# Ten orders written out, one for each pair of feature tiles, in place of two orders and a rule

## The chip, the cores and the metric

The kernel runs on one core of one Trainium2 chip. The metric is the device time of one execution in microseconds (us), lowest median best. Every engine has its own queue and runs it in order: TensorE (PE in the profile) multiplies, VectorE (DVE), ScalarE (ACT) and GpSimd (POOL) do the elementwise work, SyncE (SP) issues the transfers. Semaphores tie them together.

## The reference

The input `x` has 2048 rows of 640 numbers. Two branches are computed from it and mixed by a gate for each row:

```
g = sigmoid((x * gate_w).sum(-1))
a = linear attention of x with 32 heads of 20: learned features (two softmaxes), o = num / den, a = o @ wo
b = silu(x @ w1) @ w2          # w1: 640 x 1728, w2: 1728 x 640
out = g * a + (1 - g) * b
```

All of it is fp32. The kernel splits each operand of a product into a high and a low part in a reduced format and adds three products (high by high, high by low, low by high), so a logical product of 128 x 128 by 512 columns is three matmuls.

## The kernel before, in words

The program is straight code without a loop on the chip. It runs in three phases: keys and values of the attention with the first part of the dense branch (to about 180 us of the profile); the dense branch `b` (about 180 to 510 us); queries, attention output and mixing (the rest). The change is in the second phase.

There the rows are taken in two halves of 1024 (`h`), each of two column blocks of 512 (`j`). The 1728 features are 13 tiles of 128 and a rest. Ten of the tiles form five pairs, and each pair is computed once for each half: ten pair times, numbered `n` = 0 to 9, and the outputs of pair time n are made during pair time n + 1. Pair time 10 takes the last outputs, and one more pair of tiles beside them. In the text "pair n" is that loop index `n`, and order n belongs to it.

`pair_mm` (first layer) makes a pair with fewer products than plain multiplication: sums and differences of weight blocks and of x blocks are formed first (the weights' by `pair_weights` in the first half, stored and loaded again by `pair_weights_again` in the second). It is a generator cut into pieces, a product and what follows it on the other engines:

- P1m, P5m, P6m, P7m, Cm: products into one bank a of the accumulator memory (PSUM), line 925; P2m, P4m, P3m: products into banks b, d, c.
- P1p and P6p: a copy of bank a by ScalarE (lines 947, 969). P5m adds to the bank that P1p copies.
- P5p, P3p, P7p, Cp: sums on VectorE (957, 958, 975, 988, 989), silu on ScalarE (939), the high half (940), then the low half by VectorE or GpSimd (941). The result is `u`.

The second layer has two forms. In pair times 1 to 5 and 10, `out_items` makes ten (or five) outputs: okm is six products into a bank (line 1014), oke adds the bank to an accumulator on VectorE (1019). There are four such banks, used in turn, so the fifth product group from here must wait for this eviction. In pair time 5 each oke is followed by a product with the gate on GpSimd (1088) and a store. In pair times 6 to 9, `sevens` makes the outputs with seven products in place of eight: pieces 1am to 7bm, y0m, y1m (1055, 1077) and evictions 1ae to 7be, y0e, y1e (1043, 1045); t2, t3, t4 are differences of `u` on GpSimd (909), h and l their high and low halves on ScalarE and GpSimd (899, 903).

Between them stand the preparations, also in pieces:

- w0 to w11 (`pair_weights`): w0 loads two raw tiles; w1 and w2 make high halves on ScalarE (313, 813) and low halves on GpSimd (324, 814); w3 to w6 are sums on GpSimd (823); w7 to w10 high and low halves of these (826, 827). In the second half w0 to w3 are loads alone (840).
- c0 to c3 (`w2_loads`): load, then high half on ScalarE (313) and low half on GpSimd (324), for each of two tiles of the second layer; in the second half c0 and c1 are loads (847).
- b0 to b8 and d0 to d8 (`block_sums`): four sums on GpSimd (879), four high halves on ScalarE (884) with low halves on VectorE (885).
- xl and xu, yl and yu: a load of x on SP (639), and its halves on ScalarE and VectorE (1341, 1342). In pair 4, r0 and r1 issue four loads of x each; s10 and s11 are differences on VectorE, s20 to s41 on GpSimd (773); p10 to p41 their halves on ScalarE (777) and VectorE (778). g loads the gates.
- s0, s1 in pairs 6 to 9: loads of stored sums (894). st: the stores that are due.

All instructions of TensorE, ScalarE, VectorE and GpSimd in this phase are held in the order in which the pieces are called (`inorder`), so a piece that waits holds up all that is behind it on its engine. SP's issues are placed by the framework, by written order and by readiness in its own schedule. Tiles with one tag share a few slots: raw tiles four, weights in tag w nine.

What sets the order of the pieces: pair 0 has an order written out, `HEAD`. For pairs 6, 7 and 8 there is `SLOT`, for pair 9 `LAST`. For pairs 1 to 5 and 10 there is a rule, `pair_time` with `emit`: after each piece pair of `pair_mm` it takes so many okm, oke as a table says (`PT`, `PTS`), and before and after each of these at least two preparations, or more if otherwise they would not be through in time. Followed by hand, the rule gives for pair 1

```
P1m P1p b0 b1 o0m o0e b2 b3 P2m P2p b4 b5 o1m o1e b6 b7 P5m P5p st b8 c0 o2m o2e c1 c2 P4m P4p c3
o3m o3e d0 d1 P6m P6p d2 d3 o4m o4e d4 d5 P3m P3p d6 d7 o5m o5e d8 w0 P7m P7p w1 w2 o6m o6e w3 w4
o7m o7e w5 w6 o8m o8e w7 w8 Cm Cp w9 w10 o9m o9e w11
```

and for pair 4

```
g P1m P1p c0 r0 o0m o0e c1 r1 P2m P2p c2 o1m o1e P5m P5p st s10 c3 o2m o2e s11 P4m P4p s30 w0 o3m
o3e s31 w1 P6m P6p s20 w2 o4m o4e s21 w3 P3m P3p s40 o5m o5e s41 p10 P7m P7p p11 p40 o6m o6e p41 xl4
o7m o7e xu4 p20 o8m o8e p21 xl3 Cm Cp xu3 o9m o9e
```

## Time and profile before

| what | value |
|---|---|
| median of 3 runs | 731.88 us (731.69 to 732.32) |
| the profiled execution | 732.16 us, span in the profile 730.4 us, clock 1.000 |
| TensorE busy | 722.1 us, 99% |
| VectorE busy | 429.7 us, 59% |
| GpSimd busy | 396.0 us, 54% |
| ScalarE busy | 297.1 us, 41% |
| transfers | 98.80 MB, mean 135 GB/s |

How to read it: the span runs from the first to the last instruction that the profile holds, and the execution's own time is 1.8 us longer. A row of the timeline is the start in us from the begin of the span, the length, the engine, the line of the kernel, the operation, what it writes and reads with the shapes, how many are merged in it, and in brackets the idle time of the engine before it and what ended it. Matmuls are pipelined: a row's length contains the drain of its last one, and the step from one start to the next tells the pace. The table of windows cuts the span where one asks for it and gives each engine's busy time in each piece.

### The profile page before, as it was taken

Reading aid. Unit: us, or ns where it says so; the run is one execution under the profiler, and the core shown is the slowest. Engines: PE = TensorE matmul, PEld = TensorE weight load, DVE = VectorE, ACT = ScalarE, POOL = GpSimd, SP = SyncE. Lnnn points to the kernel's source line nnn. Section 1 sums busy time; section 2 is a strip of 40 time slices with the busy share of each in tenths; the row PEclk is TensorE's granted clock in tenths of the full one; section 3 lists DMA queues with packets and bytes.
Section 4 is the critical chain, followed back from the end, with each engine's and each line's share of the span. In section 5 each row is a group of like instructions: output and inputs, shape, how many; then the busy total and the mean of one; then the engine's idle time right before and its main releaser. Section 6 shows DMA issues by size and latency. Waiting matters only on the chain.

```text
span 730.4 us, 12517 instructions
## 1 busy us (share of the span) xinstructions
PE 722.1 (99%) x4935; PEld 621.2 (85%) x4935; DVE 429.7 (59%) x708; ACT 297.1 (41%) x558; POOL 396.0 (54%) x307
## 2 busy tenths in 40 slices
PE   9999999999999999999999999999999999999998
PEld 8888888888888878887888788788997899999988
DVE  4565555565253546568625655663887776766652
ACT  5333322336465354435354323435334453435330
POOL 2354545534756385472866548311598767777440
PEclk9999999999999999999999999999999999999999
DMA  8111111114734567786965613342133322121222
GB/s 300 61 56 56 46 56 55 63 35 136 242 116 176 208 259 239 255 318 243 382 226 180 228 65 105 97 133 73 52 110 114 111 95 80 59 91 47 74 87 80
DMA packets 50751, 98.80 MB, mean 135 GB/s; under 512 B 6352, under 2 KB 25828, under 8 KB 50692
## 3 DMA queue, kind: packets, MB, share of 16 engines
q1 hardware_dynamic: 50692, 98.00, 39.6%
q8 instruction: 39, 0.64, 0.4%
q14 instruction: 20, 0.16, 0.1%
HBM read 66.15 MB, written 31.84 MB: 134 GB/s over the span
## 4 chain that ended last, share of the span: by engine, by line
PE 87%; POOL 5%; DVE 3%; issue 2%; ACT 2%; DMA 1%; SPq 0%; DVEq 0%; POOLq 0%; ACTq 0%
PE kvp L527 17%; PE o L1014 13%; PE pa L1636 10%; PE a L925 8%; PE pq L503 7%; PE o L1055 4%; PE ph L593 3%; PE c L925 3%; PE d L925 3%; PE b L925 3%; PE pn L1594 3%; PE pT L1487 2%; PE hp L612 2%; PE kvt L514 2%; PE o_m L1077 1%
## 5 line engine op out<-in xcount | busy, mean ns | idle before, releaser
L1014 PE MATMUL o<-u,w 128*128 128x512 f32 x580 | 142.8, 391 | 0.1
L1014 PEld LDWEIGHTS o<-u,w 128*128 128x128 f32 x580 | 108.0, 188 | 23.1 <-DVE acc L1019 0.9
L527 PE MATMUL kvp<-wh,xa 128*128 128x480 f32 (+2 forms) x420 | 92.4, 360 | 0.0
L527 PEld LDWEIGHTS kvp<-wh,xa 128*128 128x128 f32 x420 | 72.8, 188 | 10.4
L324 POOL TENSOR_TENSOR w<-wr,w 128x640 fp32r<-128x640 f32 x26 | 42.0, 1619 | 72.5 <-ACT w L313 64.6
L1636 PE MATMUL pa<-oT,wo 128*128 128x256 f32 x600 | 77.0, 281 | 0.1
L1636 PEld LDWEIGHTS pa<-oT,wo 128*128 128x128 f32 x600 | 73.8, 188 | 1.1 <-DVE oT L1615 0.8
L1170 POOL TENSOR_TENSOR ez<-eq,zbc 128x1280 f32<-128x1280 f32 x16 | 48.0, 3000 | 47.9 <-DVE sm L1200 24.6
L555 POOL TENSOR_TENSOR ek<-ek,st 128x1280 f32<-128x1280 f32 x16 | 38.2, 2386 | 50.4 <-DVE st L554 42.1
L1019 DVE TENSOR_TENSOR acc<-acc,o 128x512 f32<-128x512 f32 x70 | 46.5, 680 | 16.6 <-PE o L1014 16.4
L503 PE MATMUL pq<-wq,xb 128*128 128x320 f32 x360 | 55.9, 312 | 0.0
L939 ACT ACTIVATE v<-v 128x512 f32<-128x512 f32 x33 | 20.9, 632 | 84.6 <-DVE v L958 36.7
L503 PEld LDWEIGHTS pq<-wq,xb 128*128 128x128 f32 x360 | 52.9, 188 | 2.2 <-DVE oT L1615 2.0
L155 POOL TENSOR_TENSOR xa<-xra,xa 128x512 fp32r<-128x512 f32 (+1 forms) x26 | 26.3, 1036 | 41.7 <-ACT xa L153 37.3
L527 PE MATMUL kvp<-wl,xa 128*128 128x480 f32 (+2 forms) x210 | 47.5, 356 | 0.0
L1153 ACT ACTIVATE eq<-eq 128x1280 f32<-128x1280 f32 x16 | 20.4, 1277 | 63.6 <-DVE eq L494 63.6
L941 DVE TENSOR_TENSOR u<-v,u 128x512 fp32r<-128x512 f32 x29 | 21.2, 731 | 34.5 <-ACT u L940 30.2
L360 ACT COPY v<-kvp 128x340 f32<-128x340 f32 (+1 forms) x30 | 12.5, 417 | 70.2 <-PE kvp L527 68.3
L527 PEld LDWEIGHTS kvp<-wl,xa 128*128 128x128 f32 x210 | 36.6, 188 | 4.8
L1045 DVE TENSOR_TENSOR acc<-acc,o 128x512 f32<-128x512 f32 x48 | 31.3, 684 | 12.1 <-PE o L1055 12.1
L1206 POOL TENSOR_TENSOR eq<-eq,sm 128x1280 f32<-128x1280 f32 x16 | 37.9, 2366 | 1.0 <-DVE sm L1200 0.8
L553 DVE TENSOR_REDUCE st<-ek 128x64 f32<-128x1280 f32 x16 | 23.8, 1486 | 22.7 <-ACT ek L689 21.3
(236 smaller groups left out, 1485.5 us busy)
## 6 DMA issues: line engine op xcount, KB each, us to landing
wr<-w SPq DMA_DIRECT2D x33, 320.0 KB
w_d<-w SPq DMA_DIRECT2D x15, 640.0 KB
xr<-xT SPq DMA_DIRECT2D x27, 256.0 KB
w<-w_d SPq DMA_DIRECT2D x10, 640.0 KB
fb_d<-acc SPq DMA_DIRECT2D x20, 256.0 KB
s_d<-s SPq DMA_DIRECT2D x8, 512.0 KB
sa<-s_d SPq DMA_DIRECT2D x8, 512.0 KB
y<-fb_d SPq DMA_DIRECT2D x16, 256.0 KB
```

Source lines behind the costliest of these rows:

```text
L324: eng.tensor_tensor(t[:, 1, :], r[:, :D], t[:, 0, :].bitcast(F32), op=ALU.subtract)
L503: nc.tensor.matmul(dst, xt[c][:, hx, :], w[:, c, hw, lo : lo + n], start=first, stop=(hx == 1 and c == NC - 1))
L527: nc.tensor.matmul(kv_cols(t, lo, hi), xt[c][:, hx, :], WKV[hw][:, c, w_cols(lo, hi)], start=(n == 0), stop=(n == 3 * NC - 1), skip_group_ ...
L555: nc.gpsimd.tensor_tensor(groups(e), groups(e), spread(st[:, 1, :]), op=ALU.mult)
L925: last["mm"] = nc.tensor.matmul(out, lhs, rhs, start=(first and i == 0), stop=(stop and i == len(todo) - 1), skip_group_check=True)
L1014: nc.tensor.matmul(o, lhs, rhs, start=(n == 0), stop=(n == len(todo) - 1))
L1019: nc.vector.tensor_tensor(acc[j][m], acc[j][m], o, op=ALU.add)
L1045: nc.vector.tensor_tensor(acc[j][m], acc[j][m], o, op=ALU.add)
L1055: nc.tensor.matmul(o, ws[hw], x()[hx], start=(first and i == 0), stop=(i == len(PASSES) - 1), skip_group_check=True)
L1170: nc.gpsimd.tensor_tensor(ez, Q[t]["e"], zbc, op=ALU.mult)
L1206: nc.gpsimd.tensor_tensor(groups(q["e"]), groups(q["e"]), spread(q["sm"][:, 2 * H : 4 * H]), op=ALU.mult)
L1636: nc.tensor.matmul(pa[:, a, :], wo_tile[0][:, c, hw, ds] if c < NG else WOR[:, ds], o[:, ho, c, :] if c < NG else o[:GW, ho, c, :], start= ...
```

## The change

The rule and the two orders are gone; each pair from 1 to 10 has its own order of pieces, O1 to O10, and one loop calls the pieces in that order. The set of pieces of each pair is the same, and each piece does the same work on the same engine. Engine by engine, this is what stands in another order:

- Pair 1: on ScalarE d6 ahead of P3p, w1 ahead of P7p, w9 ahead of Cp; on VectorE d4 ahead of o4e, d6 ahead of P3p.
- Pair 2: on ScalarE w1, w2 ahead of P6p and w10 ahead of P7p; on VectorE d5 ahead of o2e.
- Pair 3: o1m ahead of P2m on TensorE; xu0, xu1 ahead of c1 and d5 ahead of P6p on ScalarE; xu0 ahead of o0e, d4 and d5 ahead of o3e and d7 ahead of o4e on VectorE; the loads xl in the order 2, 1, 0.
- Pair 4: c3 ahead of P5p, p10 ahead of P3p, p11 and p40 ahead of P7p, and xu3 ahead of Cp on ScalarE; on VectorE s10 ahead of o1e, p10 ahead of P3p's sum, p11 and p40 ahead of P7p, p41 ahead of o6e, xu4 ahead of o7e, xu3 ahead of Cp; r0 and g, p20 and p21 swapped; GpSimd's part of c3 comes with it, in the same place of its queue.
- Pair 5: P5p's sums ahead of o3e, and its low half ahead of o3's product with the gate; c0 ahead of yl3 and w0, w1 ahead of st on SP.
- Pair 6: y0m ahead of P5m on TensorE; P1p ahead of 2ae and h3 ahead of 1be on ScalarE; s1 ahead of c0 on SP.
- Pair 7: P5p ahead of h4 (ScalarE), y0e (VectorE) and l3 (GpSimd); s1 and w1 ahead of c0 on SP.
- Pairs 8 and 9: no engine's order changes.
- Pair 10: yu0 ahead of o1e and yu1 ahead of P5p.

```diff
@@ -78,17 +78,56 @@
 hp10 v1 hm11 hp11 hp13 v2 p21 v3 da4 P5m P5p P4m em0 p30 y0 v4 y1 y2 ea0 P4p em1 y3 P6m y4 ea1 y5 P6p
 em2 P3m y6 y7 ea2 P3p y8 y9 P7m P7p em3 Cm ea3 y10 em4 y11 Cp ea4
 """
-SLOT = """
-s0 P1m t3 w0 2am 1bm t2 2ae P1p 1am 1be 1ae 2bm h3 P2m h2 P2p t4 l2 c0 2be P5m y0m y0e s1 w1 l3 c1 h4
-P5p P4m y1m 6am w2 P4p P6m 6bm y1e 6ae P6p l4 6be 5am w3 5bm 5ae P3m 7am 5be P3p 7ae 7bm 7be P7m 4am
-3bm 4ae 3am P7p 3ae 4bm 3be Cm 4be Cp
+O1 = """
+P1m P1p o0m b0 b1 o0e b2 b3 P2m P2p b4 b5 o1m o1e b6 b7 P5m P5p st b8 c0 o2m o2e c1 c2 c3 P4m P4p d0
+o3m o3e d1 d2 P6m P6p d3 d4 o4m o4e d5 d6 P3m P3p d7 d8 o5m o5e P7m w0 w1 P7p w2 w3 o6m o6e w4 w5 o7m
+o7e w6 w7 o8m o8e w8 w9 Cm Cp w10 w11 o9m o9e
 """
-LAST = """
-P1m t3 1am t2 s0 w0 1bm s1 P1p 1be 2am P2m 2bm c0 P2p h2 1ae l2 h3 l3 2be P5m 6am t4 w1 h4 2ae P5p w2
-y0m w3 y1m y1e 6bm w4 P4m P4p l4 P6m y0e 6ae w5 w6 w7 5am 5ae P6p P3m 6be P3p 5bm c1 w8 5be 7am P7m
-7bm 7ae 7be 3am w9 4am P7p 3ae Cm 3bm Cp w10 4ae 3be 4bm w11 4be
+O2 = """
+P1m o0m P1p c0 c1 o0e c2 c3 P2m P2p d0 d1 o1m o1e d2 d3 P5m P5p st d4 d5 o2m o2e d6 d7 P4m P4p w0 o3m
+d8 o3e w1 P6m w2 P6p w3 w4 o4m o4e w5 w6 P3m P3p w7 w8 o5m o5e w9 w10 P7m P7p w11 o6m o6e o7m o7e o8m
+o8e Cm Cp o9m o9e
+"""
+O3 = """
+xl2 xl1 P1m P1p xl0 o0m c0 xu0 o0e o1m P2m o1e xu1 P2p c1 xu2 P5m st c2 P5p c3 o2m o2e d0 d1 P4m P4p
+d2 d3 o3m d4 d5 o3e P6m P6p o4m d6 d7 o4e d8 w0 P3m P3p w1 w2 o5m o5e w3 w4 P7m P7p w5 w6 o6m o6e w7
+w8 o7m o7e w9 o8m w10 o8e w11 Cm Cp o9m o9e
+"""
+O4 = """
+r0 P1m P1p o0m g c0 o0e c1 P2m P2p r1 c2 o1m st s10 o1e c3 P5m o2m P5p o2e s11 P4m w0 P4p s30 w1 o3m
+o3e s31 w2 P6m P6p s20 w3 o4m o4e s21 s40 P3m p10 P3p o5m s41 o5e p11 p40 P7m P7p p41 xl4 o6m o6e xu4
+o7m o7e p21 p20 xl3 o8m o8e xu3 Cm Cp o9m o9e
+"""
+O5 = """
+P1m P1p p30 p31 o0m o0e yl4 yu4 o1m o1e yl2 yu2 o2m o2e P2m P2p c0 yl3 yu3 c1 o3m w0 w1 P5m P5p st w2
+w3 o3e o4m o4e P4m P4p P6m P6p o5m o5e P3m P3p o6m o6e P7m P7p o7m o7e o8m o8e Cm Cp o9m o9e
+"""
+O6 = """
+s0 P1m t3 w0 2am 1bm t2 P1p 1am 2ae 1ae 2bm h3 1be P2m st h2 P2p t4 l2 y0m y0e s1 c0 2be P5m w1 l3 c1
+h4 P5p P4m y1m 6am w2 P4p P6m 6bm y1e 6ae P6p l4 6be 5am w3 5bm 5ae P3m 7am 5be P3p 7ae 7bm 7be P7m
+4am 3bm 4ae 3am P7p 3ae 4bm 3be Cm 4be Cp
+"""
+O7 = """
+P1m t3 s0 w0 2am t2 1bm P1p 2ae 1am 1be 1ae 2bm h3 P2m st h2 s1 w1 P2p t4 l2 c0 2be P5m c1 P5p y0m
+y0e l3 h4 P4m y1m 6am w2 P4p P6m 6bm y1e 6ae P6p l4 6be 5am w3 5bm 5ae P3m 7am 5be P3p 7ae 7bm 7be
+P7m 4am 3bm 4ae 3am P7p 3ae 4bm 3be Cm 4be Cp
+"""
+O8 = """
+s0 P1m t3 w0 2am 1bm t2 2ae P1p 1am 1be 1ae 2bm h3 P2m st h2 P2p t4 l2 c0 2be P5m y0m y0e s1 w1 l3 c1
+h4 P5p P4m y1m 6am w2 P4p P6m 6bm y1e 6ae P6p l4 6be 5am w3 5bm 5ae P3m 7am 5be P3p 7ae 7bm 7be P7m
+4am 3bm 4ae 3am P7p 3ae 4bm 3be Cm 4be Cp
+"""
+O9 = """
+t3 P1m 1am 1bm 1be t2 s0 w0 s1 2am P1p P2m st P2p 2bm c0 h2 1ae l2 h3 2be P5m l3 6am t4 w1 h4 2ae P5p
+w2 y0m w3 y1m y1e 6bm w4 P4m P4p l4 P6m y0e 6ae w5 w6 w7 5am 5ae P6p P3m 6be P3p 5bm c1 w8 5be 7am
+P7m 7bm 7ae 7be 3am w9 4am P7p 3ae Cm 3bm Cp w10 4ae 3be 4bm w11 4be
+"""
+O10 = """
+P1m P1p c0 c1 o0m o0e c2 c3 P2m P2p yl0 yu0 o1m o1e yl1 yu1 P5m P5p st q0 o2m q1 o2e kb kl P4m P4p
+o3m o3e P6m P6p o4m o4e P3m P3p P7m P7p fl0 Cm Cp
 """
 NSEV = 4
+ORDERS = (HEAD, O1, O2, O3, O4, O5, O6, O7, O8, O9, O10)
 PASSES = ((0, 0), (0, 1), (1, 0))
...
-    def emit(prep, k, slots, least=1):
-        for _ in range(max(least, -(-len(prep) // max(slots, 1)))):
-            if prep and prep[0][0] <= k:
-                prep.pop(0)[1]()
-
-    def pair_time(d1, d2, prep, counts):
-        slots = len(counts) + sum(counts)
-        for k, n in enumerate(counts):
-            twice(d1)
-            if k == 2:
-                store()
-            for i in range(n + 1):
-                emit(prep, k, slots, 2)
-                slots -= 1
-                if i < n:
-                    twice(d2)
-        run(d1)
-        emit(prep, len(counts), 1)
-        assert not prep
...
-    PT = (1, 1, 1, 1, 1, 1, 3, 1)
-    PTS = {NPAIR - 1: (3, 1, 1, 0, 1, 1, 2, 1), 2 * NPAIR - 2: (1, 1, 1, 1, 1, 0, 0, 0)}
...
-            prep = thunks((w2_again if again else w2_loads)(2 * p, 2 * p + 1), 5)
-            if NPAIR - 2 < n + 1 < 2 * NPAIR - 2:
-                prep += thunks(pair_weights_again(n + 1), 5)
-            elif n + 1 < 2 * NPAIR - 1:
...
+            q = (n - 1) % (NPAIR - 1)
+            ops["st"] = store
+            named(MM, pair_mm(n, h))
             if NPAIR - 1 < n < NPAIR + NSEV:
+                sevens(q, n == NPAIR)
+                named("s0 s1", sums_again(q))
+                for i in range(1, 4):
+                    ops[f"t{i + 1}"] = lambda i=i, q=q: t_sum(q, i)
+                    ops[f"h{i + 1}"] = lambda i=i, q=q: t_hi(q, i)
+                    ops[f"l{i + 1}"] = lambda i=i, q=q: t_lo(q, i)
+            else:
+                d2 = out_items(int(n > NPAIR - 1), (2 * q, 2 * q + 1), end=n == NPAIR - 1)
+                named(" ".join(f"o{k}m o{k}e" for k in range(2 * NC if n < 2 * NPAIR - 2 else NC)), d2)
+            if NPAIR - 2 < n < 2 * NPAIR - 2:
+                named("c0 c1", w2_again(2 * p, 2 * p + 1))
+            else:
+                named("c0 c1 c2 c3", w2_loads(2 * p, 2 * p + 1))
+            if NPAIR - 3 < n < 2 * NPAIR - 3:
+                named("w0 w1 w2 w3", pair_weights_again(n + 1))
+            elif n < 2 * NPAIR - 2:
+                named(" ".join(f"w{k}" for k in range(12)), pair_weights(n + 1))
             if n == 1:
+                named(" ".join(f"b{k}" for k in range(9)), block_sums(0))
             if n < NSEV:
+                named(" ".join(f"d{k}" for k in range(9)), block_sums(n))
             if n == NPAIR - 3:
+                new_chunks(0, "x", {c: lambda k=k: place(k) for c, k in ((0, 8), (1, 9), (2, 11))})
             if n == NPAIR - 2:
+                ops["g"] = lambda: load_gates(0)
+                for cc in range(2):
+                    ops[f"r{cc}"] = lambda cc=cc: half_raws(cc)
+                    for i in range(1, 5):
+                        eng = nc.vector if i == 1 else nc.gpsimd
+                        ops[f"s{i}{cc}"] = lambda i=i, cc=cc, eng=eng: x_sum(i, XR[cc], eng)
+                    for i in (1, 2, 4):
+                        ops[f"p{i}{cc}"] = lambda i=i, cc=cc: x_part(i, cc, XR[cc])
+                new_chunks(0, "x", {4: slot_of(0, 4), 3: lambda: place(10)})
             if n == NPAIR - 1:
+                for cc in range(2):
+                    ops[f"p3{cc}"] = lambda cc=cc: x_part(3, cc, XR[cc])
+                new_chunks(1, "y", {c: slot_of(1, c) for c in (4, 2, 3)})
             if n == 2 * NPAIR - 2:
-            pair_time(pair_mm(n, h), d2, prep, PTS.get(n, PT))
+                new_chunks(1, "y", {c: slot_of(1, c) for c in range(2)})
+                named("q0 q1", reg_loads())
+                ops.update(kb=load_b_consts, kl=kvm_load, fl0=lambda: load_fused(0))
+            for name in ORDERS[n].split():
+                ops.pop(name)()
+            assert not ops, list(ops)
```

More of the change, by code (lines that the diff above doesn't have):

```diff
@@ L1414, in mix_kernel, with new_chunks, slot_of @@
         assert not ops
-        late = []
-        for c in range(2):
-            late += x_new(c, 1, lambda c=c: slot(f"xf_3_{c}"))
-        def slot_time(n, p, q, h):
-            named("P1m P1p P2m P2p P5m P5p P4m P4p P6m P6p P3m P3p P7m P7p Cm Cp", pair_mm(n, h))
-            sevens(q, n == NPAIR)
-            named("s0 s1", sums_again(q))
-            named("c0 c1", w2_again(2 * p, 2 * p + 1))
-            for i in range(1, 4):
-                ops[f"t{i + 1}"] = lambda i=i: t_sum(q, i)
-                ops[f"h{i + 1}"] = lambda i=i: t_hi(q, i)
-                ops[f"l{i + 1}"] = lambda i=i: t_lo(q, i)
-            if n < 2 * NPAIR - 3:
-                named("w0 w1 w2 w3", pair_weights_again(n + 1))
-            else:
-                named(" ".join(f"w{k}" for k in range(12)), pair_weights(n + 1))
-            for name in (SLOT if n < 2 * NPAIR - 3 else LAST).split():
-                ops.pop(name)()
-                if name == "P2m":
-                    store()
-            assert not ops, list(ops)
+        MM = "P1m P1p P2m P2p P5m P5p P4m P4p P6m P6p P3m P3p P7m P7p Cm Cp"
+        def new_chunks(j, names, where):
+            for c in where:
+                (_, load), (_, use) = x_new(c, j, where[c])
+                ops[f"{names}l{c}"], ops[f"{names}u{c}"] = load, use
+        def slot_of(j, c):
+            return lambda: slot(f"xf_{2 + j}_{c}")
         for n in range(1, 2 * NPAIR - 1):
```

43 lines of the change are left out of this document (removed).

## The prediction

> **What bounds the kernel now.** The page of the profile comes first: TensorE is busy 99% of the span at full clock, and it holds most of the chain of work that ended last.
>
> ```profile
> span 730.4 us, 12517 instructions
> ...
> PE 722.1 (99%) x4935; PEld 621.2 (85%) x4935; DVE 429.7 (59%) x708; ACT 297.1 (41%) x558; POOL 396.0 (54%) x307
> ...
> PEclk9999999999999999999999999999999999999999
> ...
> PE 87%; POOL 5%; DVE 3%; issue 2%; ACT 2%; DMA 1%; SPq 0%; DVEq 0%; POOLq 0%; ACTq 0%
> ```
>
> A change of order on the other engines can therefore win only what TensorE waits. Busy time is modelled and hides short waits, so the second view is the table of windows, one for each pair, cut where the first product of a pair starts (pairs 2, 3, 4, 5, 6, 7, 8, 9). Columns: span of the window, then busy time and count of each engine, granted clock, DMA share, GB/s.
>
> ```profile
> 257.64:284.71 27.07, 26.43 (x115) 21.24 (x114) 15.89 (x26) 13.26 (x28) 23.40 (x26) 1.00 0.75 271
> 284.71:310.55 25.84, 25.84 (x115) 21.40 (x114) 15.47 (x26) 10.57 (x21) 10.07 (x10) 1.00 0.64 222
> 310.55:336.39 25.84, 25.84 (x115) 21.40 (x114) 15.99 (x23) 9.79 (x19) 16.75 (x15) 1.00 0.82 310
> 336.39:362.87 26.48, 26.42 (x115) 21.24 (x114) 19.38 (x31) 12.39 (x24) 14.52 (x11) 1.00 0.84 312
> 362.87:387.66 24.79, 24.79 (x109) 20.19 (x108) 9.15 (x14) 11.35 (x20) 17.34 (x14) 1.00 0.75 252
> 387.66:412.78 25.12, 25.02 (x109) 20.11 (x108) 14.17 (x21) 9.41 (x17) 12.79 (x11) 1.00 0.54 179
> 412.78:438.01 25.23, 25.13 (x109) 20.04 (x108) 14.80 (x23) 8.44 (x15) 12.87 (x11) 1.00 0.34 119
> 438.01:463.73 25.72, 25.40 (x109) 20.04 (x108) 15.27 (x25) 10.75 (x21) 16.50 (x16) 1.00 0.28 88
> ```
>
> Pairs 1 to 5 have 114 products each (a cut counts one more). Pairs 3 and 4 need 25.84 us, 0.2267 us a product: TensorE never waits there. Pair 2 is 27.07 - 25.84 = 1.23 us longer, pair 5 26.48 - 25.84 = 0.64. Pairs 6 to 9 have 108 products, 24.48 us by that step, and lose 0.31, 0.64, 0.75 and 1.24. All ten pairs together thus offer some 4.8 us, and the orders decide how much of it.
>
> **Pair 2, from what order 1 moves.** TensorE's timeline (start, length, line; the last two rows are for pair 5, below) shows two waits in pair 2: its first product P1m takes 1.89 us where six products back to back read 1.52 (342.47), and P5m starts late, released by P1p, ScalarE's copy of bank a (L947).
>
> ```profile
> 257.64 1.89 PE L925 MATMUL a<-xf,w 128*128 128x512 f32 x6
> ...
> 264.86 1.66 PE L925 MATMUL a<-xo,wb 128*128 128x512 f32 x6 [0.55 <-ACT v L947]
> ...
> 337.98 4.66 PE L1014 MATMUL o<-u,w 128*128 128x512 f32 x18
> 342.47 1.52 PE L925 MATMUL b<-xo,wf 128*128 128x512 f32 x6
> ```
>
> The rows behind it, of ScalarE, GpSimd and VectorE in turn (start, length, line):
>
> ```profile
> 251.74 0.71 ACT L884 CAST s<-wr 128x256 fp32r<-128x256 f32 x2
> 255.84 0.62 ACT L940 CAST u<-v 128x512 fp32r<-128x512 f32 x1
> 256.37 0.72 ACT L313 CAST w<-wr 128x640 fp32r<-128x640 f32 x1
> 257.00 0.51 ACT L813 CAST wb<-wr 128x384 fp32r<-128x384 f32 x1
> 262.19 0.41 ACT L826 CAST wc<-wr 128x256 fp32r<-128x256 f32 x1 [1.23 <-POOL wr L823]
> 264.21 0.59 ACT L947 COPY v<-a 128x512 f32<-128x512 f32 x1
> ```
>
> ```profile
> 257.17 1.57 POOL L324 TENSOR_TENSOR w<-wr,w 128x640 fp32r<-128x640 f32 x1 [7.87 <-PE o L1014]
> 258.70 1.02 POOL L814 TENSOR_TENSOR wb<-wr,wb 128x384 fp32r<-128x384 f32 x1
> ```
>
> ```profile
> 249.84 0.68 DVE L975 TENSOR_TENSOR v<-v,c 128x512 f32<-128x512 f32 x1
> ...
> 252.48 0.75 DVE L885 TENSOR_TENSOR s<-wr,s 128x256 fp32r<-128x256 f32 x2
> 253.15 0.68 DVE L1019 TENSOR_TENSOR acc<-acc,o 128x512 f32<-128x512 f32 x1
> 253.75 0.68 DVE L988 TENSOR_TENSOR v<-v,a 128x512 f32<-128x512 f32 x1
> ```
>
> P1m's fifth product needs the low half of the new weights, which GpSimd makes at 257.17 to 258.74 (piece w1) after 7.87 us of idleness, because ScalarE makes the high half only at 256.37, behind P7p. Order 1 puts w1 ahead of P7p. But it also puts o4e and d6 ahead of P3p on VectorE: by the steps from start to start, 0.60 (253.15 to 253.75) and 0.33 (half of 252.48 to 253.15), P3p's add moves from 249.84 to 250.77, by 0.93. ScalarE's two steps of P3p move with it, and the casts behind them, from 251.74 to 252.67; there d7 stands alone (half of 0.71), and w1 starts at about 253.0, its part on GpSimd 0.80 later (256.37 to 257.17) at 253.8, done by 255.4. P1m's wait, 1.89 - 1.52 = 0.37, goes.
>
> Then the second wait. P7p is later by 0.93 - 0.33 = 0.60 (d6 has left its way), so its cast L940 starts at 256.44, and w2 follows at once (step 0.53) at 256.97, about where it was. GpSimd, though, is no longer held by w1: w2's low half starts when the cast is done (0.51, and 0.08 as at 257.17), at 257.56 in place of 258.70, and the chain of sums behind it moves by 1.14. So w8 comes at 261.05, and the same six pieces stand from there to P1p, which ends at 264.80 - 1.14 = 263.66. P5m is released 0.06 later, at 263.72; TensorE wants it after 27 products, at 257.64 + 6.12 = 263.76. Margin 0.04. So all of 1.23 can go, and nothing more; if P1p is late by x, x and about 0.1 of restart come back. If w1's slot or raw tile were not free at 253.0, nothing would go. A loss is not to be had from these moves: what P7p makes is wanted at 257.64 + 1.36 at the earliest and is there at about 257.8. I take **-1.2 us**, bounds 0 and -1.23.
>
> **Pair 5, from what order 4 moves.** TensorE's second group of products (o0m) starts at 337.98 in place of 336.39 + 1.36 = 337.75, and loses more before 342.47. It waits for banks: VectorE empties the bank of o6 at 337.25 to 337.93 and that of o8 at 340.25 to 340.93, because it is behind.
>
> ```profile
> 327.82 0.69 DVE L975 TENSOR_TENSOR v<-v,c 128x512 f32<-128x512 f32 x1 [1.42 <-PE c L925]
> 329.86 1.20 DVE L941 TENSOR_TENSOR u<-v,u 128x512 fp32r<-128x512 f32 x1 [1.35 <-ACT u L940]
> ...
> 331.58 1.18 DVE L778 TENSOR_TENSOR xo<-xr,xo 128x512 fp32r<-128x512 f32 x1
> 332.68 0.68 DVE L988 TENSOR_TENSOR v<-v,a 128x512 f32<-128x512 f32 x1
> ...
> 337.25 0.68 DVE L1019 TENSOR_TENSOR acc<-acc,o 128x512 f32<-128x512 f32 x1
> ...
> 340.25 0.68 DVE L1019 TENSOR_TENSOR acc<-acc,o 128x512 f32<-128x512 f32 x1
> ```
>
> ```profile
> 315.38 1.60 POOL L324 TENSOR_TENSOR w<-wr,w 128x640 fp32r<-128x640 f32 x1
> 321.74 2.05 POOL L324 TENSOR_TENSOR w<-wr,w 128x640 fp32r<-128x640 f32 x1 [4.76 <-ACT w L313]
> 323.75 5.51 POOL L773 TENSOR_TENSOR xr<-xr,xr 128x512 f32<-128x512 f32 x4
> 329.20 3.02 POOL L773 TENSOR_TENSOR xr<-xr 128x512 f32<-128x512 f32 x2
> ```
>
> Order 4 moves p10 (331.58) into VectorE's idle 1.42 us ahead of P3p's add, and p11 and p40 from behind P7p to ahead of it. Behind P7p stands then one piece fewer, 0.60, before both banks: o6e ends at 337.33 and o8e at 340.33, against 337.75 and 340.48 wanted, and the 0.64 goes. That holds if P7p stays in its place. Ahead of it p11 and p40 (1.20) take the room of p10, which took 1.10 (331.58 to 332.68) since it ran beside GpSimd's subtractions. If p11 is stretched as p10 was, P7p is 0.60 late and the gain is nothing. GpSimd decides: its six subtractions end at 332.22 now. Order 4 puts c3 ahead of P5p, so that L324 (321.74) can follow at 316.98, and the subtractions can start when their loads have landed, which no row shows. By the table, 310 GB/s ran in pair 4, and the loads and one store up to there (2.7 MB) are 8.7 us at that rate from their first issue at 311.88: about 320.6, an estimate, against some 325.1 at which the second subtraction starts now (323.75 + 5.51/4). Two us earlier would do to clear p11 (from 331.6). I take **-0.5 us**, bounds 0 and -0.64.
>
> The Trainium skill says on the page "SBUF — State Buffer", section "Who interferes with whom", that a VectorE instruction with two SBUF inputs and a GpSimd one that reads SBUF exclude each other for the whole of the instruction. The two stretched rows agree: the one from 331.58 ends at 332.76, 0.54 after GpSimd's last at 332.22, and the other rows (0.68 to 0.69) have one input in PSUM or GpSimd idle beside them.
>
> **The other edits, each at nothing.** The products keep their order but for two swaps, o1m with P2m in pair 3 and y0m with P5m in pair 6, whose inputs are all there in pairs that show no wait at those places. Pair 3's P1p, c1 and casts: it has no wait to win, and the banks that its late evictions hold are wanted only four groups later. Pair 2's P6p behind w1 and w2: 1.2 us on ScalarE, against a bank used a whole P3m and o5m later (2.04 + 1.36). Pair 5's P5p ahead of o3e swaps two pieces of VectorE and one gate product on GpSimd; its SP order brings the reloads for pair 6 forward by one or two places, wanted 17 us later. Pair 6's 1be behind h3 and pair 7's P5p ahead of h4, l3 and y0e delay pieces by at most one GpSimd subtraction each. Orders 8 and 9 leave every engine's order as it was. Pair 10's loads are only brought ahead of P5p. So the 0.31 to 1.24 us of pairs 6 to 9 stay. SP's queue is not ordered by hand; I take it to run as now.
>
> **The sum.** -1.2 - 0.5 = -1.7 us. It reaches the end, since the phase behind is released by TensorE:
>
> ```profile
> 510.04 2.60 PE pq L503 x18
> ...
> 517.60 2.98 POOL ez L1170
> ```
>
> The profiled execution took 732.16 us (1.8 outside its span) and the median of the runs is 731.88: **730.2 us**, -0.23%. A run of this kernel can tell about 0.2%, 1.46 us, from no change (730.42 to 733.34).
>
> **Rivals.**
> - Only pair 2 gains: p11 is stretched beside GpSimd, or the loads land late. For it speaks that VectorE is at its busiest there (19.38 us in pair 5), against it c3's 4.76 us of idle room. 731.88 - 1.2 = 730.7. By that page of the Trainium skill ("SBUF — State Buffer", "Who interferes with whom") it comes so wherever the subtractions still run at 331.6.
> - Only P1m's wait goes in pair 2: o4e ahead of P3p costs more than 0.93 and the 0.04 of margin is gone; with pair 5, 731.88 - 0.4 - 0.5 = 731.0.
> - No change, 731.9: w1 waits on ScalarE for its slot at 253.0 and the same pieces end as late as now.
> - Slower: p40 stands ahead of P7p on ScalarE and VectorE and needs GpSimd's fifth subtraction, which ends at about 330.7 (half of 3.02 behind 329.20). Counted back from the wanted 337.75 over the 5.95 us from there to o6e (0.66 + 0.64, then 332.68 to 337.93 less 0.60), it may end at 331.8. If SP puts the four stores (2 MB, 6.6 us at 310 GB/s) ahead of the second half of the loads, it ends near 335.6: 3.8 us of wait where 0.64 was, 731.88 - 1.2 + 3.2 = 733.9. It decides the sign by over 0.2% from 335.1 on. For it: the store piece is written earlier and the DMA share is 0.82. Against: the loads stand ahead of the store in the order still.
>
> **How the numbers follow.** Forecast 0.56 (own range 729.8 to 730.6), pair 2 alone 0.16, P1m alone 0.09, no change 0.07, slower 0.12. The range reaches from 729.4, where pair 6 to 9 give a little too, to 732.0, past no change; it leaves out the slower case. Faster by over 0.2%: the forecast less its edge, 0.54; slower 0.12; within 0.34.
>
> **What would show it.** Right: the window of pair 2 at 25.8 to 25.9 us, w1's L324 on GpSimd before 255, P5m without a wait; the window of pair 5 at 25.8 to 26.0, GpSimd's subtractions done before 331.6 in this profile's terms; pairs 6 to 9 as now within 0.1. Wrong: a wait inside pairs 1, 3 or 4, a late L778 ahead of P7p, or an SP row of a load that moved behind a store.

## The result, and the profile after

The changed kernel takes 730.30 us (median of 13 runs, 729.96 to 731.36), the kernel before, run beside it, 731.74 (13 runs, 731.05 to 732.99): a ratio of 0.9981, 95% interval 0.9973 to 0.9990. It is faster by 0.19%, some 1.4 us; 730.2 was forecast. The profiled execution took 730.17 us.

The page of the profile looks as before: TensorE at 99%; of the chain of work that ended last it holds 97% (87% before).

```profile
PE 721.2 (99%) x4935; PEld 621.0 (85%) x4935; DVE 429.9 (59%) x708; ACT 297.4 (41%) x558; POOL 395.6 (54%) x307
```

The table of windows of the changed kernel, cut at the first product of pairs 2 to 10 as in the prediction, shows the change (span of the window, busy time and count of each engine, clock, DMA share, GB/s):

```profile
257.30:283.36 26.06, 26.06 (x116) 21.32 (x114) 16.52 (x27) 13.37 (x28) 22.17 (x25) 1.00 0.75 278
283.36:309.20 25.84, 25.84 (x116) 21.40 (x114) 15.92 (x27) 10.56 (x21) 10.65 (x11) 1.00 0.63 224
...
335.04:361.21 26.17, 26.17 (x115) 21.24 (x114) 18.46 (x30) 11.64 (x22) 14.53 (x11) 1.00 0.91 332
...
436.32:461.95 25.63, 25.36 (x109) 20.04 (x108) 15.25 (x25) 10.74 (x21) 16.45 (x16) 1.00 0.31 88
```

Pair 2 went from 27.07 to 26.06 us (-1.01), pair 5 from 26.48 to 26.17 (-0.31). Pairs 3 and 4 stand at 25.84 as before; pairs 6 to 9 are 24.81, 25.08, 25.22 and 25.63, moved by +0.02, -0.04, -0.01 and -0.09. From the first product of pair 1 to that of pair 10 it is 230.49 us, where it was 231.93: -1.44. The span fell by 2.0 (730.4 to 728.4), but 0.34 of that lies ahead of pair 1, where nothing was changed: over the profiles of this study pair 1 begins anywhere from 231.26 to 232.14. The windows repeat better than a whole execution: pairs 3 and 4 take 25.83 to 25.85 in every profile of this study, and pair 2 with order 1 of the change 26.01 to 26.09 in eight. Pair 5 is the exception. In the run below that alters pairs 6 to 8 only, with all pieces and SP's issues ahead of pair 5 in the same order as here, it is 26.36 and not 26.17, so its -0.31 holds for one profile and is not sure to better than 0.2. What follows goes by the windows.

TensorE's timeline in pair 2 and at the begin of pair 5 (start, length, line):

```profile
257.30 1.52 PE L964 MATMUL a<-xf,w 128*128 128x512 f32 x6
...
263.50 1.66 PE L964 MATMUL a<-xo,wb 128*128 128x512 f32 x6
...
336.40 4.57 PE L1053 MATMUL o<-u,w 128*128 128x512 f32 x18
```

P1m takes 1.52 us, the 0.37 of waiting is gone. P5m starts at 263.50; 27 products behind 257.30 would be 263.42, so 0.08 of its wait is left. In pair 5 the three groups of products take 4.57 us from start to the end of the last, where an undisturbed group of 18 is 18 x 0.2267 and a drain of 0.16, 4.24.

The engines behind pair 2, GpSimd and then ScalarE (lines are 39 higher than before):

```profile
253.46 1.58 POOL L363 TENSOR_TENSOR w<-wr,w 128x640 fp32r<-128x640 f32 x1 [4.48 <-ACT w L352]
257.23 1.11 POOL L853 TENSOR_TENSOR wb<-wr,wb 128x384 fp32r<-128x384 f32 x1 [2.20 <-ACT wb L852]
258.42 0.74 POOL L862 TENSOR_TENSOR wr<-wr 128x256 f32<-128x256 f32 x1
```

```profile
252.66 0.72 ACT L352 CAST w<-wr 128x640 fp32r<-128x640 f32 x1
...
256.64 0.51 ACT L852 CAST wb<-wr 128x384 fp32r<-128x384 f32 x1
```

The begin of pair 2 is 0.34 earlier than before, so 0.34 is to be taken off the prediction's times. w1's cast was forecast at 253.0 - 0.34 = 252.66 and stands at 252.66; w1's low half at 253.8 - 0.34 = 253.46, and stands there; w2's cast at 256.97 - 0.34 = 256.63, and stands at 256.64; w2's low half at 257.22, and stands at 257.23. When it starts, VectorE is still at P7p's low half, which reads two inputs in SBUF:

```profile
256.77 0.69 DVE L980 TENSOR_TENSOR u<-v,u 128x512 fp32r<-128x512 f32 x1 [1.35 <-ACT u L979]
```

Behind pair 5, GpSimd's last five subtractions and VectorE:

```profile
322.59 4.24 POOL L812 TENSOR_TENSOR xr<-xr,xr 128x512 f32<-128x512 f32 x3 [4.09 <-DMA xr<-xT]
326.79 2.56 POOL L812 TENSOR_TENSOR xr<-xr 128x512 f32<-128x512 f32 x2
```

```profile
328.44 1.46 DVE L980 TENSOR_TENSOR u<-v,u 128x512 fp32r<-128x512 f32 x1 [1.35 <-ACT u L979]
...
330.42 1.28 DVE L817 TENSOR_TENSOR xo<-xr,xo 128x512 fp32r<-128x512 f32 x2
331.62 0.68 DVE L1027 TENSOR_TENSOR v<-v,a 128x512 f32<-128x512 f32 x1
...
335.58 0.68 DVE L1058 TENSOR_TENSOR acc<-acc,o 128x512 f32<-128x512 f32 x1
...
338.58 0.68 DVE L1058 TENSOR_TENSOR acc<-acc,o 128x512 f32<-128x512 f32 x1
```

Counted from the begin of pair 5 (336.39 before, 335.04 now), o6e ends at 1.22 in place of 1.54 and o8e at 4.22 in place of 4.54: 0.32 earlier, not 0.60. p11 and p40 run unstretched (two in 1.28), but P3p's low half takes 1.46 us beside GpSimd's last subtraction, and that subtraction is late because the second of the six waits for a load until 322.59.

### The profile page after: what moved, and what is told of

Same layout as the page of the kernel before. It is cut to its first block, busy times and chain, and to the rows that moved or that the text cites. A ratio compares the mean times of both kernels' runs of the same rounds, so it can differ in the third digit from the quotient of the medians.

```text
span 728.4 us, 12513 instructions
## 1 busy us (share of the span) xinstructions
PE 721.2 (99%) x4935; PEld 621.0 (85%) x4935; DVE 429.9 (59%) x708; ACT 297.4 (41%) x558; POOL 395.6 (54%) x307
## 4 chain that ended last, share of the span: by engine, by line
PE 97%; DVE 1%; ACT 1%; DMA 1%; issue 0%; DVEq 0%; ACTq 0%
PE o L1053 18%; PE kvp L566 17%; PE pa L1629 10%; PE pq L542 9%; PE a L964 9%; PE o L1094 5%; PE ph L632 3%; PE c L964 3%; PE b L964 3%; PE d L964 3%; PE pn L1587 3%; PE pT L1480 2%; PE hp L651 2%; PE kvt L553 2%; PE o_m L1116 1%; PE kvp L440 1%
## 5 line engine op out<-in xcount | busy, mean ns | idle before, releaser
L566 PEld LDWEIGHTS kvp<-wh,xa 128*128 128x128 f32 x420 | 72.8, 188 | 10.4
L399 ACT COPY v<-kvp 128x340 f32<-128x340 f32 (+1 forms) x30 | 12.5, 417 | 70.1 <-PE kvp L566 68.2
```

The source lines that it names most:

```text
L566: nc.tensor.matmul(kv_cols(t, lo, hi), xt[c][:, hx, :], WKV[hw][:, c, w_cols(lo, hi)], start=(n == 0), stop=(n == 3 * NC - 1), skip_group_ ...
```

## The experiments

The theory: order 1 gives pair 2's gain by w1 ahead of P7p, less what the moves of d4 and d6 cost; order 4 gives pair 5's by fewer pieces of VectorE ahead of two evictions, as far as GpSimd's subtractions are out of the way; the other eight orders give nothing. Rivals: other orders have a part in it; the moves of d4 and d6 cost nothing; the loads of pair 4 set GpSimd's end whatever the order. In each table of windows only the rows that decide are shown. For a single execution the whole time varies by about a microsecond (the kernel before, run beside them, showed 731.20 and 732.13), so it decides nothing: order 1 alone took 731.12 and order 4 alone 731.41 beside 731.20, and the 1.0 and 0.3 us that I expected of these two times do not show in them.

**Order 1 alone.** Orders 2 to 10 as before.

```diff
 O1 as in the change
-O2 to O10 of the change
+O2 to O10 as the rule, SLOT and LAST gave them
```

> Order 1 alone, all other pairs as before. If the whole gain of pair 2 comes from order 1, as predicted: window of pair 2 at 26.06 us as with the whole change (27.07 before), P1m without a wait, P5m at most 0.2 late; pair 5 stays at 26.48, pairs 6 to 9 as before; time about 1.0 us under before. Rival, that orders 2 and on have a part in it: pair 2 stays over 26.3.

Its windows of pairs 2 and 5:

```profile
257.52:283.57 26.05, 26.05 (x116) 21.32 (x114) 16.52 (x27) 13.26 (x28) 22.37 (x25) 1.00 0.77 281
...
335.25:361.75 26.50, 26.43 (x116) 21.24 (x114) 19.38 (x31) 12.39 (x24) 14.52 (x11) 1.00 0.82 303
```

Order 1 gives pair 2's gain alone, 1.02 us, and nothing in pair 5.

**Order 4 alone.** The same with O4 of the change and all others as before.

> Order 4 alone. If pair 5's 0.31 us come from order 4, as predicted: window of pair 5 at 26.17 (26.48 before), pair 2 at 27.07 as before, time about 0.3 under before. Rival, that it is order 5 with P5p's sums ahead of o3e: pair 5 stays at 26.48.

```profile
336.40:362.24 25.84, 25.84 (x115) 21.40 (x114) 17.86 (x29) 11.05 (x21) 14.56 (x11) 1.00 0.90 323
```

Neither expectation: pair 5 comes to 25.84, the whole 0.64 gained (pair 2 stays at 27.09). So order 4 by itself is worth twice what the change's profile shows of it, and something else in the change takes half of it back. SP's queue shows a difference. In the changed kernel, then with order 4 alone:

```profile
312.37 0.38 SPq L830 DMA_DIRECT2D w_d<-wb  x1
312.85 0.38 SPq L830 DMA_DIRECT2D w_d<-wc  x1
313.32 4.78 SPq L678 DMA_DIRECT2D xr<-xT  x4
```

```profile
313.74 0.38 SPq L830 DMA_DIRECT2D w_d<-wb  x1
314.61 3.03 SPq L678 DMA_DIRECT2D xr<-xT  x4
317.72 0.44 SPq L830 DMA_DIRECT2D w_d<-wc  x1
```

The change issues the store of wc (512 KB) ahead of the second half of pair 4's loads; with order 4 alone, as in the kernel before, it comes behind. The second subtraction then starts at 323.37 of a pair that begins at 310.56, 12.81 us into it; in the change at 322.59 - 309.20 = 13.39.

**Which order moves the store.** The change with order 3 as before; with it, the store of wc is behind the loads again.

```diff
-O3 of the change
+O3 as the rule gave it
 O1, O2, O4 to O10 of the change
```

> The changed kernel, with order 3 as before. In the changed kernel SP issues the store of wc ahead of the second half of pair 4's loads, with order 4 alone behind it; there the second subtraction starts 12.81 us into pair 4 in place of 13.40, P3p's low half takes 0.86 in place of 1.46, and pair 5 needs 25.84 in place of 26.17. SP places its issues by readiness, and with order 3 the weights of pair 4 are made earlier. If that is the cause, order 3 as before brings the store back behind the loads: second subtraction at 12.8, P3p's low half at about 0.9, pair 5 at 25.84. Rival, that the loads' landing only varies with the length of pair 2 or from run to run: 13.4 and 26.17 as with the change.

Pair 5, and in pair 4 (which begins at 309.53) GpSimd's last five subtractions, P3p's low half and P7p's sum:

```profile
335.37:361.21 25.84, 25.84 (x116) 21.40 (x114) 17.76 (x28) 11.05 (x21) 14.52 (x11) 1.00 0.93 335
```

```profile
322.23 3.80 POOL L812 TENSOR_TENSOR xr<-xr,xr 128x512 f32<-128x512 f32 x3 [3.59 <-DMA xr<-xT]
325.98 3.00 POOL L812 TENSOR_TENSOR xr<-xr 128x512 f32<-128x512 f32 x2
```

```profile
328.77 0.76 DVE L980 TENSOR_TENSOR u<-v,u 128x512 fp32r<-128x512 f32 x1 [1.35 <-ACT u L979]
...
331.25 0.68 DVE L1027 TENSOR_TENSOR v<-v,a 128x512 f32<-128x512 f32 x1
```

The second subtraction starts 12.70 us into the pair, P3p's low half takes 0.76, P7p stands 0.70 earlier in the pair than in the change (21.72 against 22.42), and pair 5 waits for nothing. Order 3, whose pieces I had costed at nothing, takes back 0.33 us, and it does so one pair later and over SP's queue. What it does to the order of SP's issues is sure: the store of wc stands ahead of the second half of the loads in all eight profiles that have order 3 of the change and leave SP to the framework, and behind it in all five that have order 3 as before. That only the store of wc makes the difference is not shown by this run, since order 3 moves other pieces too.

**The stores bound behind the loads.** The change with all its orders; only the issues of two stores are tied to the last load of x.

```diff
-        with tc.issue_after(last["mm"].ins):
-            while stores:
-                d, t = stores.pop(0)
-                nc.sync.dma_start(d, t.bitcast(F32))
+        while stores:
+            d, t = stores.pop(0)
+            late = any(d is x for x in w_d[NPAIR - 2][1:3])
+            with tc.issue_after(last["x" if late else "mm"].ins):
+                nc.sync.dma_start(d, t.bitcast(F32))
```

> The changed kernel, with the two stores wb and wc of pair 4's weights bound behind the second half of the loads on SP (one load of x, xl4, then comes ahead of them: 0.92 MB less ahead of the loads). If transfers ahead in the queue hold the landing: 0.92 MB at 310 GB/s is 3.0 us, so the second subtraction starts at about 10.4 us into pair 4 (13.40 with the change), the subtractions end at 17.3 (20.15), P3p's low half takes 0.7 (1.46), pair 5 at 25.84 (26.17). Rival, that the loads are held by the slots they wait for: second subtraction later than 12.5.

Pair 5, SP's queue, GpSimd and VectorE (pair 4 begins at 309.08; lines behind the edit are one higher still):

```profile
334.93:360.76 25.83, 25.83 (x115) 21.39 (x114) 17.69 (x28) 10.97 (x21) 14.51 (x11) 1.00 0.93 336
```

```profile
310.41 4.47 SPq L678 DMA_DIRECT2D xr<-xT  x9
314.94 0.42 SPq L831 DMA_DIRECT2D w_d<-wb  x1
```

```profile
321.62 3.79 POOL L812 TENSOR_TENSOR xr<-xr,xr 128x512 f32<-128x512 f32 x3 [3.55 <-PE o L1054]
```

```profile
320.80 0.68 DVE L812 TENSOR_TENSOR xr<-xr 128x512 f32<-128x512 f32 x1
```

With every piece in the change's order, the place of two stores on SP, and of one load of x (xl4) that SP then also issues ahead of them, brings pair 5 to 25.83: the loss is in the queue of the transfers. The last of the four loads is issued by 5.80 us into the pair, by 7.08 with order 4 alone and by 8.90 in the change, so it is not the slots that hold them. The size I gave it was wrong: the second subtraction starts 12.54 us into the pair, not 10.4 (over the rival's 12.5, though not for the rival's reason), and is no longer released by a transfer. It overwrites a block that VectorE's subtraction (L812, 320.80 to 321.48) reads, and follows it by 0.14. So about 0.9 us is all that earlier loads can give there while VectorE's subtraction stays where it is.

**The store piece later.** The same question, asked by moving the piece that calls the stores.

```diff
-... r1 c2 o1m st s10 o1e c3 P5m o2m P5p o2e s11 P4m w0 ...
+... r1 c2 o1m s10 o1e c3 P5m o2m P5p o2e s11 P4m st w0 ...
```

> The changed kernel, with the stores of order 4 put behind P4m. In the changed kernel two stores (1.18 MB) are issued ahead of the second half of the loads, which lands at 322.43, and the second subtraction starts right behind, at 322.59. If these stores hold the loads: they land 1.18 MB at 310 GB/s earlier, 3.8 us, the subtractions end at about 325.5 to 326, ahead of P3p's low half, which takes 0.7 in place of 1.46; P7p is 0.75 earlier and pair 5 comes to 25.84. Rival, that the loads are late for the slots they wait for, or that the transfers share the rate anyhow: landing at 321 or later, pair 5 at 26.1 to 26.2.

The stores of wb and wc stayed where they were, at 312.51 and 312.98, ahead of the loads: the place of st in the order does not place them. The run tells nothing on the question it was made for. The second subtraction came still later than in the change (323.18, 13.85 us into pair 4, which begins at 309.33), and yet pair 5 came to 25.92, by another way, of which VectorE shows this:

```profile
328.57 0.69 DVE L980 TENSOR_TENSOR u<-v,u 128x512 fp32r<-128x512 f32 x1 [1.35 <-ACT u L979]
...
329.78 1.80 DVE L817 TENSOR_TENSOR xo<-xr,xo 128x512 fp32r<-128x512 f32 x2
```

P3p's low half met GpSimd between two subtractions and took 0.69; p11 and p40 took 1.80 in place of 1.28. P7p's sum stands 22.17 us into the pair, 0.25 earlier than in the change, and that is what pair 5 won.

**c3 back behind P5p.** The change, with c3 of order 4 at its old place.

```diff
-... st s10 o1e c3 P5m o2m P5p o2e s11 P4m ...
+... st s10 o1e P5m o2m P5p o2e s11 c3 P4m ...
```

> The changed kernel, with c3 of order 4 back behind P5p and s11. By the prediction GpSimd's six subtractions then wait for c3's low half, which comes about 4 us later, and end some 1.8 us later (331.2 in place of 329.35); VectorE's p11 is stretched by them as well as P3p's low half, P7p comes 0.3 to 0.5 later: window of pair 5 at 26.4 to 26.7. Rival, that the landing of the second half of the loads (322.43) sets the subtractions anyhow: 26.17 as with the change.

```profile
335.72:362.25 26.53, 26.42 (x115) 21.24 (x114) 18.83 (x30) 12.00 (x23) 14.53 (x11) 1.00 0.90 326
```

```profile
328.58 3.00 POOL L812 TENSOR_TENSOR xr<-xr 128x512 f32<-128x512 f32 x2
```

Pair 5 is at 26.53, no better than before (26.48): with GpSimd's subtractions ending at 331.58, 21.70 us into the pair (21.67 before), the other moves of order 4 win nothing. That c3 had to move was in the prediction, and it is so.

**o6e and o8e one place earlier.** The change, with p41 behind o6e and p20 behind o8e.

```diff
-... P7m P7p p41 xl4 o6m o6e xu4 o7m o7e p21 p20 xl3 o8m o8e xu3 ...
+... P7m P7p xl4 o6m o6e p41 xu4 o7m o7e p21 xl3 o8m o8e p20 xu3 ...
```

> The changed kernel, with p41 behind o6e and p20 behind o8e in order 4. If VectorE's place of these evictions is all that holds the products of pair 5: o6e and o8e end 0.60 earlier, o8e at 338.66 in place of 339.26, wanted at 339.12; pair 5 at 25.84. Rival, that p41 and p20 are wanted soon: a new wait at P4m or P6m of pair 5 and a window of 26.0 or more.

```profile
334.95:360.79 25.84, 25.84 (x115) 21.34 (x114) 18.59 (x30) 11.77 (x22) 14.52 (x11) 1.00 0.89 325
```

As expected: two places on VectorE are worth the 0.33 too, with the loads no earlier than in the change (the second subtraction starts 13.52 us into pair 4, P3p's low half takes 1.57).

**w1 alone.** The kernel before with one piece moved.

```diff
-... d6 d7 o5m o5e d8 w0 P7m P7p w1 w2 o6m ...
+... d6 d7 o5m o5e d8 w0 P7m w1 P7p w2 o6m ...
```

> Before, and of order 1 one move alone: w1 ahead of P7p (d4, d6 and the rest where they were). By the prediction's steps P3p's add is then not 0.93 late and P7p not 0.60 late: w2's low half on GpSimd starts 0.59 behind its cast at 256.37, so at 256.96 against 258.70 before, P1p ends 1.74 earlier, at 263.06, ahead of the 263.76 at which P5m is wanted. Pair 2 at 25.84, 1.23 us gained, more than with the whole of order 1. Rival, that something else holds P1p at that place (its own place behind Cp, w9 and w10): 26.0 to 26.1 as with the whole order.

```profile
257.10:282.94 25.84, 25.84 (x115) 21.40 (x114) 15.96 (x26) 13.26 (x28) 22.04 (x25) 1.00 0.78 284
```

```profile
256.43 1.11 POOL L853 TENSOR_TENSOR wb<-wr,wb 128x384 fp32r<-128x384 f32 x1 [2.23 <-ACT wb L852]
```

Pair 2 has no wait left: one move of the kernel before is worth 1.23 us, 0.22 more than the whole of order 1. Against the begin of pair 2, w2's low half starts at -0.67, where it stood at -0.07 in the change.

**All of order 1 but w1.** The change with w1 back behind P7p.

```diff
-... P7m w0 w1 P7p w2 w3 o6m ...
+... P7m w0 P7p w1 w2 w3 o6m ...
```

> The changed kernel, with w1 put back behind P7p in order 1; the moves of d4, d6 and w9 stay. By the prediction's steps the moves of d4 and d6 alone cost: P7p 0.60 later, w1's cast 0.60 later, P1m's wait 0.97 in place of 0.37, P1p 0.60 later; P5m is released 1.70 behind its time (1.10 before), pair 2 at 27.6 to 27.7. Rival, that these moves cost nothing: pair 2 at 27.07. Pair 5 at 26.17 in both cases.

```profile
231.71:257.67 25.96, 25.96 (x115) 21.21 (x113) 12.82 (x24) 10.48 (x22) 9.21 (x11) 1.00 0.60 213
257.67:285.23 27.56, 26.57 (x115) 21.35 (x115) 16.39 (x27) 13.72 (x29) 23.64 (x26) 1.00 0.72 264
```

```profile
257.67 1.20 PE L964 MATMUL a<-xf,w 128*128 128x512 f32 x4
259.31 0.73 PE L964 MATMUL a<-xf,w 128*128 128x512 f32 x2 [0.44 <-POOL w L363]
259.88 1.55 PE L1053 MATMUL o<-u,w 128*128 128x512 f32 x6
```

P1m begins 0.12 late (pair 1 is that much longer than 25.84) and its fifth product 0.73 late (259.31 less 257.67 and 4 x 0.2267); with the restart the next group is 0.97 late (259.88, wanted at 231.71 + 25.84 + 1.36 = 258.91), the wait that was expected. Pairs 1 and 2 together are 1.84 over 51.68, where 1.83 follows from the expectation's steps (1.70 and 0.13 of restart). Without w1's move order 1 costs 0.61 us (53.52 for both pairs, 52.91 before), which is what the prediction had for d4 and d6; that it is theirs alone rests on these steps, since the run keeps w9's move too.

**The other eight orders.** The change with orders 1 and 4 as before.

> The changed kernel with orders 1 and 4 as before: what the other eight orders do by themselves. By the prediction nothing: pair 2 at 27.07, pair 5 at 26.48, the others as before; 0.1 us at most under before (pairs 7 and 9 are 0.04 and 0.09 shorter in the changed kernel). Rival, that part of pair 2 or 5 comes from orders 2, 3 or 5: pair 2 under 26.9 or pair 5 under 26.4.

Pairs 2 and 5, and two of SP's rows in pair 4:

```profile
257.71:284.78 27.07, 26.48 (x115) 21.24 (x114) 15.91 (x26) 13.36 (x28) 23.15 (x26) 1.00 0.73 271
...
336.46:362.95 26.49, 26.44 (x116) 21.25 (x114) 19.37 (x31) 12.49 (x24) 14.52 (x11) 1.00 0.87 306
```

```profile
314.27 0.38 SPq L830 DMA_DIRECT2D w_d<-wc  x1
314.75 4.41 SPq L678 DMA_DIRECT2D xr<-xT  x4
```

731.90 us (10 runs) against 731.72 of the kernel before (15 runs), a ratio of 1.0003 (0.9993 to 1.0012): no difference. They do nothing by themselves. The store of wc is ahead of the loads here too, but without order 4 GpSimd is at c3's low half until 323.85 and the loads are not what it waits for; order 3's cost shows only where order 4 has made the loads matter.

**6bm ahead of P6m in pairs 6 to 8**, an addition to the change, with 6be ahead of P6p:

```diff
-... 6am w2 P4p P6m 6bm y1e 6ae P6p l4 6be 5am ...
+... 6am w2 P4p 6bm P6m y1e 6ae l4 6be P6p 5am ...
```

> The changed kernel, with 6bm ahead of P6m and 6be ahead of P6p in orders 6, 7 and 8. The wait of 5bm for the eviction 6be (0.27, 0.38 and 0.38 with its restart) is what these pairs lose in the middle. If nothing else stands behind it: pair 6 at 24.5, pair 7 at 24.7, pair 8 at 24.85 (24.81, 25.08, 25.22 with the change), about 1.0 us less. Rival, that the wait only moves to the next product or to P6p's bank: pairs as with the change within 0.1.

```profile
361.61:386.09 24.48, 24.48 (x109) 20.27 (x108) 9.16 (x14) 11.54 (x20) 17.33 (x14) 1.00 0.76 242
386.09:410.78 24.69, 24.69 (x109) 20.20 (x108) 14.14 (x21) 9.32 (x17) 12.72 (x11) 1.00 0.54 183
```

With pair 8 at 24.83, 1.1 us in three pairs, as expected. In pair 6 of the change the nine products 6bm, 5am and 5bm took 2.50 us where nine without a wait take 2.20; with P6m also between 6bm and 5bm, which needs 6bm's bank again, no group there is longer than without a wait. Pair 5, whose order this edit leaves alone, is 26.36 in this profile (the table at the end has its reason).

**All three together**: order 1 as before with w1 ahead of P7p, order 4 with o6e and o8e earlier, orders 6 to 8 with 6bm ahead.

> The changed kernel with three orders altered as the looks so far advise: order 1 as before but for w1 ahead of P7p; order 4 with p41 behind o6e and p20 behind o8e; orders 6 to 8 with 6bm ahead of P6m and 6be ahead of P6p. If the three gains add: pair 2 at 25.84 (26.06 with the change), pair 5 at 25.84 (26.17), pairs 6 to 8 at 24.48, 24.69, 24.83 (24.81, 25.08, 25.21); 1.65 us under the change, 728.6 to 728.8, and 3.0 us under before, a ratio of 0.996. Rival, that pair 5 or pair 6 gets a new wait from the earlier start: 729.2 or more.

```profile
257.53:283.37 25.84, 25.84 (x115) 21.40 (x114) 16.79 (x26) 13.36 (x28) 21.55 (x25) 1.00 0.78 289
...
335.05:360.94 25.89, 25.89 (x115) 21.39 (x114) 18.52 (x30) 11.79 (x22) 14.51 (x11) 1.00 0.89 322
```

729.08 us (median of 5 runs, 728.64 to 730.09), a ratio of 0.9966 to before (0.9954 to 0.9979). The nine windows sum to 228.90 us, 3.03 under before and 1.59 under the change; the median is 1.22 under the change's, 0.3 above the 728.6 to 728.8 that I expected, and the two intervals against before (0.9973 to 0.9990 for the change) still overlap by a little. By the windows it beats both kernels; by the times alone it beats the kernel before.

## Why the prediction was right

**Pair 2, -1.2 forecast, -1.01 measured.** The mechanism and its steps hold: the path over P3p, d7, w1, P7p and w2 was met within 0.02 us at each piece. What failed is the last of it: P5m "released 0.06 later, at 263.72", with a margin of 0.04. P5m came 0.08 late, and with the restart 0.22 is lost, the case of the sentence "if P1p is late by x, x and about 0.1 of restart come back". The term that was mis-sized is w2's low half: from its start to the next sum is 1.19 us (257.23 to 258.42), where I had moved the row of before with its 1.10. The instruction itself takes 1.11 us in place of 1.02: in its new place it starts 0.23 ahead of the end of P7p's low half on VectorE (256.77 to 257.46). Over the profiles of before and after it takes 1.01 to 1.03 wherever no VectorE instruction with two inputs in SBUF runs at its start and 1.11 to 1.20 where one does, which reads as the same exclusion of the two engines that the prediction had used for pair 5 and not looked for here; no run tests it by itself. With w1 alone moved, the piece meets VectorE in the same way and takes the same 1.11, and there the margin is large enough to cover it. The margin was 0.04 on a chain of some ten pieces, and I took the forecast to its full side.

**Pair 5, -0.5 forecast, -0.31 measured.** Right was that the order of VectorE's pieces in pair 4 holds two banks of pair 5, that p11 is clear of the subtractions, and that c3 decides it. The step that failed is "that holds if P7p stays in its place": P7p is 0.29 late, since P3p's low half takes 1.46 us (1.20 before) and p11 with p40 1.20 in place of p10's 1.10, less 0.07 that P3p begins earlier. I had asked of GpSimd only to be done before p11, not before P3p's low half, which stands ahead of P7p as well. Behind that failed "SP's queue is not ordered by hand; I take it to run as now": a new order on the compute engines reordered the transfers, the store of wc went ahead of the loads, and half the gain of order 4 went with it. The estimate for the landing, about 320.6 in the times of before, was 3 us too early: in the change the second subtraction is released by its load at 322.59, which is 323.94 there. The store's place is only some 0.6 of that (with order 4 alone it starts 12.81 us into the pair, 323.36 there). And 320.6 was out of reach whatever the loads did: VectorE's s11 reads the block that this subtraction overwrites, and ends 12.4 us into the pair, 322.95 there, which the prediction did not count.

**The other orders at nothing.** Right for themselves, by the run with these alone. Wrong for order 3 in company with order 4, at 0.33 us by the two profiles compared: its pieces were costed on the compute engines alone, not on SP. Pair 9 is at 25.62 to 25.67 in all ten profiles with orders 6 to 10 of the change (as they are, or with 6bm moved), and at 25.69 to 25.74 in the four without; in the two profiles of before and after the difference sits at one product, 2.26 us into the pair before and 2.18 after. Why this is so is open, as no compute engine's order changed there.

**The rivals.** "Slower", with p40 waiting for late subtractions behind stores, did not happen, but its mechanism was the right place to look: SP did put a store ahead of the loads, one of 0.5 MB and not four. Its price was too high by its own rows: a landing at 320.6 + 6.6 = 327.2 and four subtractions behind it (5.5) put the end of the fifth at 332.7, 0.9 behind the 331.8 that it may take, and not at 335.6. "Only pair 2 gains" is what the run with c3 back shows: 26.53. "Only P1m's wait goes" named the right weak point with the wrong size.

**Its own signs.** Of the signs of being right, w1's early L324, the subtractions done before 331.6 (330.70 in those terms) and pairs 6 to 9 within 0.1 came; the windows of 25.8 to 25.9 and 25.8 to 26.0 did not (26.06 and 26.17), nor P5m without a wait. And one sign of being wrong came: the row of a load that moved behind a store.

**The sum.** -1.7 forecast, -1.44 measured over the windows as well as between the medians taken side by side (731.74 and 730.30). Pair 2 gave 0.19 less and pair 5 0.19 less, and the pairs taken at nothing 0.12 more. That the forecast time was within 0.1 us of the median owes something to luck: the kernel before measured 0.14 lower than the median I started from, and the pairs taken at nothing gave 0.12. The stated range, 729.4 to 732.0, would have held no change as well.

## What to carry to other kernels

Where one engine is at 99%, cut its timeline into periods of known work and read the gain from their lengths: a change of 1 us in 730 is clear there to less than 0.1 where a pair's waits repeat (pair 2), and to 0.2 where they hang on when a load lands (pair 5), while the whole time of an execution varies by about one. Follow a moved piece along the in-order queues to the next piece that someone waits for, and compare the margin there with the scatter of the pieces in between: 0.04 us over ten pieces is no margin. And when a queue is placed by the framework from readiness, a new order on the other engines is a new order there too: look at it again, above all behind a heavy stretch of transfers.
